# Windowed attention and a gated MLP on one core: casts of later pairs placed one slot sooner, and another order of the work at the head of two blocks

## The chip, the cores and the metric

The kernel runs on one core of a Trainium2 chip. A core has a matrix engine (PE, with its weight loads listed apart as PEld), three engines for elementwise work (DVE, ACT, POOL) and SP, which here only issues DMAs. Each engine works through its own queue in order, and the queues wait for each other by semaphores. The metric is the device time of one execution in microseconds (us); lower is better.

## The reference

Attention over 4 batches of 8 heads, 768 positions, head width 64, where a query sees the 128 latest positions and the first 4 ("sinks"); then, on the 512 columns that the heads make up together, a gated MLP whose gate mixes positions.

```python
scores = scale * np.matmul(q, k.transpose(0, 1, 3, 2))
keep = is_sink | in_window
scores = np.where(keep, scores, -1000000000.0)
a = np.exp(scores - max); a = a / (sum(a) + 1e-09)
x = heads_side_by_side(np.matmul(a, v))              # 4 x 768 x 512
h = gelu_tanh(x @ w_in)                              # 4 x 768 x 1024
u, v = h[..., :512], h[..., 512:]
v_n = (v - mean(v)) / np.sqrt(var(v) + 1e-06) * g_ln
v_s = np.einsum('ts,bsd->btd', w_sg, v_n) + b_sg[None, :, None]
out = x + (u * v_s) @ w_out
```

## The kernel before

The work is cut into 16 pairs of heads (numbered n; pair n belongs to batch n // 4) and 4 blocks of MLP, one for each batch b. In every batch there are six position tiles of 128.

For a pair, `load_all` brings k and q of pair n and v of pair n - 1 from memory through SP; `cast` (L101) turns them into bf16 on POOL; `columns` (L215) turns k and q so that the head width lies on partitions, with six PE transposes and a copy by ACT or DVE, while for the pairs from 12 on `columns_by_dma` (L228) has the DMA engines do it, issued by SP. `score` (L251) makes three groups of scores (g = 0, 1, 2), each one PSUM tile of two banks and one exponential on ACT. `keep_band` (L283) zeroes what lies outside the window: group 0 by a product with a mask on DVE, groups 1 and 2 by two selects each on POOL. `values` (L307) multiplies by v on PE, and DVE divides by the row sums into x. `turn_x` (L354) transposes x on PE and copies the result to xT by ACT or DVE; `turn_x_by_dma` does it by DMA. The scores and the products with v of a pair share two PSUM buffers (`ps_s`); all else that PE makes goes round four banks (`ps_m`).

For a block, `open_v` (L380) does three quarters of the product for one tile of the MLP's v half ahead of time, `hidden_v` (L390) the last quarter, the gelu on ACT and the batch statistics on DVE; `hidden_u` (L401) does the u half. Then DVE computes an inverse root in thirteen small steps and `normalise` (L436) writes vn. `hidden` (L594) runs six units of v and eight of u, with steps of other pairs placed after named units; unit numbers count from 0, so `LAST` is the last u unit. It leaves fourteen "fillers" behind: eight of `spatial` (L443; six products on PE, two DVE operations) and six of `project` (L475), one for each tile t. A projection's four products go to one bank, and the residual x is added either by DVE, or, for the tiles in `by_act`, by a fifth product with the identity on PE with a copy by ACT; SP sends the result out.

The order of everything is written by hand, as a string (`ORDER`, L723) and a table of steps placed inside the blocks (`INSIDE`, L718). The order in which steps stand there is the order of each engine's queue. The letters: `S n g..` scores, `m n g..` masks, `AV n` values, `KA`/`QA`/`QV n` columns of k or q with the copy on ACT or DVE, `TD n` columns by DMA, `XA`/`XV n` turn x with the copy on ACT or DVE, `XD n` by DMA, `ck`/`cq`/`cv n` casts on POOL, `L n` loads, `F c` the next c fillers, `O b j` open a tile of v of block b, `B b` the block's `hidden`. A "slot" below is the stretch from one pair's `S n 0 1` to the next pair's. k_bf, q_bf, kT and qT have two buffers each, the raw loads three of each kind, the exponentials three.

Of the kernel before, what the change touches and what calls it, by code (L numbers as in the profile page):

```python
# [18 lines left out]
def kernel(  # L19
# [14 lines left out]
    nc = tc.nc  # L34
    V, G, A = nc.vector, nc.gpsimd, nc.scalar

    B, H, S, Dh = q.shape
# [6 lines left out]
    HP = H // 2  # L44
# [103 lines left out]
    for i in range(WARM):  # L148
# [3 lines left out]
        out=halves[:, :, 0, :], in_=halves[:, :, 0, :], compare_op=ALU.is_ge, fill=DARK,  # L152
        base=0, pattern=[[0, 2], [1, 128]], channel_multiplier=-1)
    G.affine_select(
        out=halves[:, :, 1, :], in_=halves[:, :, 1, :], compare_op=ALU.is_ge, fill=DARK,
# [53 lines left out]
    def bank(shape, dtype, name):  # L209
        return ps_m.tile(shape, dtype, name=name, tag="m")  # L210

    kTs, qTs, exps, avs = {}, {}, {}, {}
    x_sb, xT = {}, {}
# [166 lines left out]
    def open_v(b, j, cs=range(KD - 1)):  # L380
        if j == 0 and 0 in cs:
            v_alls[b] = work.tile([128, NT, DF], F32, name="v_all", tag="v_all", bufs=1)
            mvs[b] = small.tile([128, NT, 2], F32, name="mv", bufs=2)
        if (b, j) not in hvs:
            hvs[b, j] = bank([128, 512], F32, "hv")
        for c in cs:
            nc.tensor.matmul(hvs[b, j], xT[b][:, c, 128 * j:128 * (j + 1)],  # L387
                             w_in_sb[:, c, DF:], start=(c == 0), stop=False)

    def hidden_v(b, j):  # L390
        if (b, j) not in hvs:
            open_v(b, j)
        h_ps, c = hvs.pop((b, j)), KD - 1
        nc.tensor.matmul(h_ps, xT[b][:, c, 128 * j:128 * (j + 1)],  # L394
                         w_in_sb[:, c, DF:], start=False, stop=True)
        A.activation(out=v_alls[b][:, j, :], in_=h_ps, func=AF.Gelu_apprx_tanh)  # L396
        st = small.tile([128, 6], F32, name="st")
        V.bn_stats(out=st, in_=v_alls[b][:, j, :])  # L398
        V.bn_aggr(out=mvs[b][:, j, :], in_=st)

    def hidden_u(b, f, n):  # L401
        if f == 0 and n == 0:
            uTs[b] = work.tile([128, KU, S], BF16, name="uT", bufs=1)
        h_ps = bank([128, 512], F32, "hu")
        for c in range(KD):
            nc.tensor.matmul(h_ps[:, 0:NH], w_in_sb[:, c, 128 * f:128 * (f + 1)],  # L406
                             xT[b][:, c, NH * n:NH * (n + 1)],
                             start=(c == 0), stop=(c == KD - 1))
        A.activation(out=uTs[b][:, f, NH * n:NH * (n + 1)],  # L409
                     in_=h_ps[:, 0:NH], func=AF.Gelu_apprx_tanh)  # L410
# [25 lines left out]
    def normalise(b, j):  # L436
        if j == 0:
            vns[b] = work.tile([128, NT, DF], BF16, name="vn", bufs=1)
        V.tensor_scalar(out=vns[b][:, j, :], in0=v_alls[b][:, j, :],  # L439
                        scalar1=mvs[b][:, j, 0:1], scalar2=rstds[b][:, j:j + 1],  # L440
                        op0=ALU.subtract, op1=ALU.mult)
# [30 lines left out]
                A.copy(o_sb, o_ps[:, 0:m])  # L472
            (nc.sync if eng is V else A).dma_start(out=out[b, rows, cols], in_=o_sb)

    def project(b, t, by_act):  # L475
        rows = slice(128 * t, 128 * (t + 1))
        o_ps = bank([128, 512], F32, "o_ps")
        o_sb = small.tile([128, DM], F32, name="o_sb", bufs=6)
        for c in range(KU):
            nc.tensor.matmul(o_ps, gTs[b][:, c, rows], w_out_sb[:, c, :],  # L480
                             start=(c == 0), stop=(c == KU - 1 and not by_act))
        if not by_act:
            V.tensor_add(o_sb.rearrange("p (h d) -> p h d", h=HP),
                         o_ps.rearrange("p (h d) -> p h d", h=HP), x_sb[b][:, :, t, :])
        else:
            nc.tensor.matmul(o_ps.rearrange("p (h d) -> p h d", h=HP), iden, x_sb[b][:, :, t, :],  # L486
                             start=False, stop=True)
        if by_act:
            A.copy(o_sb, o_ps)  # L489
        nc.sync.dma_start(out=out[b, rows, :], in_=o_sb)  # L490


    LEAST, MOST = 1e-20, 1e20
# [93 lines left out]
    fillers = []  # L587

    def fill(count=1):
        for _ in range(count):  # L590
            if fillers:
                fillers.pop(0)()

    def hidden(b, between):  # L594
        units = [lambda j=j: hidden_v(b, j) for j in range(NT)]
        units += [lambda f=f, n=n: hidden_u(b, f, n) for n in range(2) for f in range(KU)]
        after = {NT + 1: [lambda: inverse_root(b)]}
        for j in range(NT):
            after.setdefault(NT + 1 + j, []).append(lambda j=j: normalise(b, j))
        for i, unit in enumerate(units):  # L600
            unit()
            for step in after.get(i, []) + between.get(i, []):
                step()
        gate = [[lambda f=f, n=n: spatial(b, f, n) for f in range(KU)] for n in range(2)]
        if b < B - 1:
            fillers.extend(gate[0] + gate[1])
            by_act = (3, 5) if b == 0 else (5,) if b < B - 2 else (1, 3, 5)
            order = (0, 2, 4, 1, 3, 5) if b < B - 2 else (1, 0, 2, 3, 4, 5)
            fillers.extend(lambda t=t: project(b, t, t in by_act) for t in order)
            return  # L610

        rows = [lambda t=t: project(b, t, t != HT) for t in range(NT - 1)]
        fillers.extend(gate[0] + [gate[1][0], rows[0], gate[1][1], gate[1][2], rows[1],
                                  gate[1][3]] + rows[2:])
        fillers.append(lambda: project_last(b, NT - 1))
# [85 lines left out]
    for j in range(3):  # L701
# [12 lines left out]

    LAST = NT + 2 * KU - 1
    INSIDE = {  # L718
        1: {2: "AV 8", 5: "KA 9", 6: "L 12, L 13", 7: "QA 9", 9: "XD 8",
            LAST: "S 9 0 1, F 1, QV 10, F 1"},  # L720
        2: {2: "AV 12", 6: "L 15, L 16", 9: "XD 12", LAST: "S 13 0 1, F 2"},
    }
    ORDER = """  # L723
        S 4 0 1, W 3 4 5, m 4 0 1, F 1, KA 5, QV 5, F 1, S 4 2, m 4 2, ck 6, cq 6, cv 5, F 1,
# [2 lines left out]
        L 9, S 6 0 1, m 6 0 1, F 1, KA 7, AV 5, S 6 2, m 6 2, F 1, QA 7, ck 8, cq 8, cv 7, F 1,  # L727
        XV 5,
        L 10, S 7 0 1, m 7 0 1, F 1, KA 8, AV 6, QA 8, S 7 2, m 7 2, ck 9, cq 9, cv 8, F 1,
        L 11, S 8 0 1, m 8 0 1, XV 6, F 1, AV 7, S 8 2, m 8 2, ck 10, cq 10, cv 9,  # L730
        O 1 0, O 1 1, XV 7, O 1 2, B 1,
        m 9 0 1, F 1, KA 10, F 1, S 9 2, m 9 2, ck 11, cq 11, cv 10, F 1,
        S 10 0 1, m 10 0 1, F 1, AV 9, XD 9, S 10 2, m 10 2, ck 12, cq 12, KA 11, TD 12, L 14,
        F 1, QA 11, cv 11, F 1,
        S 11 0 1, m 11 0 1, F 1, AV 10, S 11 2, m 11 2, ck 13, cq 13, TD 13, F 1, cv 12, F 1,
        XV 10,
        S 12 0 1, m 12 0 1, F 1, AV 11, S 12 2, m 12 2, ck 14, cq 14, TD 14, F 1, cv 13, F 1,
        O 2 0, O 2 1, XV 11, O 2 2, B 2,
        ck 15, cq 15, m 13 0 1, F 2, S 13 2, m 13 2, TD 15, cv 14, F 1,
        S 14 0 1, m 14 0 1, F 1, AV 13, XD 13, S 14 2, m 14 2, F 1, cv 15, F 1,  # L740
        S 15 0 1, m 15 0 1, F 1, AV 14, S 15 2, m 15 2, F 1, G, F 1
    """

    def run(order):
        for step in order.split(","):
            op, *n = step.split()
            n = [int(i) for i in n]
            if op == "S":
                score(*n)
            elif op == "m":  # L750
                for g in n[1:]:
                    keep_band(n[0], g, V if g == 0 else G)
            elif op == "F":
                fill(n[0])
            elif op == "AV":
                values(n[0], 0, 1)
            elif op in ("ck", "cq", "cv"):
                cast(n[0], op[1], G)
            elif op in ("KA", "QA", "KV", "QV"):
                columns(n[0], op[0].lower(), A if op[1] == "A" else V)  # L760
            elif op == "TD":
                columns_by_dma(n[0])
            elif op == "XD":
                turn_x_by_dma(n[0])
            elif op in ("XV", "XA"):
                turn_x(n[0], A if op == "XA" else V)
            elif op == "L":
                load_all(n[0])
            elif op == "W":
                for si in n:  # L770
                    turn_weights(si, V)
            elif op == "O":
                open_v(*n)
            elif op == "G":
                draw_gelu()
            else:
                assert op == "B"
                hidden(n[0], {i: [lambda o=o: run(o)] for i, o in INSIDE[n[0]].items()})

    run(ORDER)  # L780
    values(NP - 1, 0)
    fill()
# [8 lines left out]
    hidden(B - 1, {2: [lambda: seen.update(c=count_good())],  # L791
                   LAST: [lambda: fill(3)]})
    seen["t"] = total(seen["c"])
# [41 lines left out]
```

## Time and profile before

| | us |
|---|---|
| median of 3 runs | 166.66 (166.65 to 174.25) |
| the profiled execution | 166.74 |
| its span, first to last instruction | 165.0 |
| DVE busy | 131.0 |
| ACT busy | 108.6 |
| POOL busy | 78.6 |

The mean granted PE clock was 0.997 of full speed. In a row of the timeline stand the start, the busy time, the engine, the line and operation, what it writes and reads, and how many instructions are merged in it; brackets give the engine's idle time before it and what ended that. A row of SP tells when SP issued a DMA and how long it was held there, not when the data landed. A row of the waits has the sum, the number and the longest of a group of waits. Busy times of PE overlap: a matmul's end is modelled, so the distance between starts tells the rate. Some matmul records are missing.

### The profile page before, as it was taken

Reading aid. Unit: us, or ns where it says so; the run is one execution under the profiler, and the core shown is the slowest. Engines: PE = TensorE matmul, PEld = TensorE weight load, DVE = VectorE, ACT = ScalarE, POOL = GpSimd, SP = SyncE. Lnnn points to the kernel's source line nnn. Section 1 sums busy time; section 2 is a strip of 40 time slices with the busy share of each in tenths; the row PEclk is TensorE's granted clock in tenths of the full one; section 3 lists DMA queues with packets and bytes.
Section 4 is the critical chain, followed back from the end, with each engine's and each line's share of the span. In section 5 each row is a group of like instructions: output and inputs, shape, how many; then the busy total and the mean of one; then the engine's idle time right before and its main releaser. Section 6 shows DMA issues by size and latency. Waiting matters only on the chain.

```text
span 165.0 us, 4407 instructions
## 1 busy us (share of the span) xinstructions
PE 152.3 (92%) x1734; PEld 90.7 (55%) x1752; DVE 131.0 (79%) x302; ACT 108.6 (66%) x147; POOL 78.6 (48%) x113
## 2 busy tenths in 40 slices
PE   3899999999999999999999899999999999999950
PEld 3555574666576655565566456553565645555430
DVE  6787975996899978799778965989999859997520
ACT  3189888889968796698878285679548457511220
POOL 6568771206899979500299997023775000000000
PEclk9999999999999999999999999999999999999998
DMA  4999979999999999999602699999626310050352
GB/s 136 333 346 248 203 107 274 212 316 310 294 232 309 306 315 360 267 214 216 132 30 52 131 237 107 343 225 217 179 48 52 127 68 0 0 190 6 126 183 89
DMA packets 60195, 31.11 MB, mean 189 GB/s; under 512 B 48356, under 2 KB 57080, under 8 KB 60168
## 3 DMA queue, kind: packets, MB, share of 16 engines
q1 hardware_dynamic: 56800, 27.47, 70.1%
q0 software_dynamic: 2944, 2.77, 10.3%
q10 hardware_dynamic: 424, 0.53, 0.9%
q8 instruction: 15, 0.25, 0.6%
q14 instruction: 12, 0.10, 0.2%
HBM read 24.81 MB, written 6.29 MB: 188 GB/s over the span
## 4 chain that ended last, share of the span: by engine, by line
PE 68%; DVE 15%; POOL 5%; ACT 4%; issue 3%; DMA 2%; ACTq 0%; POOLq 0%
PE vs L449 16%; PE hu L406 10%; PE o_ps L480 8%; PE hv L387 7%; PE sc L267 6%; PE av L331 5%; ACT ex L281 3%; PE hv L394 3%; PE kps L219 2%; DVE st L398 2%; PE xps L358 2%; PE qps L219 2%; DVE vn L439 2%; DVE x L343 2%; DVE vsink L160 2%
## 5 line engine op out<-in xcount | busy, mean ns | idle before, releaser
L281 ACT ACTIVATE ex<-sc 128x1024 bf16<-128x1024 f32 x48 | 47.6, 1024 | 17.4 <-PE sc L277 7.4
L449 PE MATMUL vs<-wsgT,vn 128*128 128x384 bf16 x192 | 36.1, 327 | 0.4
L298 POOL TENSOR_SCALAR_AFFINE_SELECT ex<-ex 128x512 bf16<-128x512 bf16 x24 | 16.1, 670 | 21.1 <-ACT ex L281 19.3
L449 PEld LDWEIGHTS <-vn 128*128 128x128 bf16 x192 | 17.2, 98 | 13.2 <-DVE vn L439 1.5
L480 PE MATMUL o_ps<-w_out_sb,gT 128*128 128x512 bf16 x83 | 22.5, 380 | 0.5
L107 POOL CAST k_bf<-k_sb 128x768 bf16<-128x768 f32 x15 | 12.9, 861 | 20.4 <-DMA k_sb<-in_k_dram 15.5
L452 DVE SCALAR_TENSOR_TENSOR gv<-vs,g_sb,b_bc 128x384 bf16<-128x384 f32 x32 | 19.6, 611 | 3.4 <-PE vs L449 2.7
L406 PE MATMUL hu<-xT,w_in_sb 128*128 128x384 bf16 x128 | 22.1, 326 | 0.0
L396 ACT ACTIVATE v_all<-hv 128x512 f32<-128x512 f32 x24 | 13.2, 599 | 9.1 <-PE hv L394 9.0
L398 DVE BATCH_NORM_STATS2 st<-v_all 128x6 f32<-128x512 f32 x24 | 16.1, 669 | 3.5 <-ACT v_all L396 3.5
L387 PE MATMUL hv<-w_in_sb,xT 128*128 128x512 bf16 x67 | 18.2, 379 | 0.3 <-issue 0.2
L409 ACT ACTIVATE uT<-hu 128x384 bf16<-128x384 f32 x32 | 15.7, 492 | 4.1 <-PE hu L406 3.7
L267 PE MATMUL sc<-qT,kT 64*128 64x256 bf16 (+2 forms) x384 | 16.1, 256 | 1.9 <-DMA qT<-q_bf 0.8
L290 DVE TENSOR_TENSOR ex<-ex,mask 128x1024 bf16<-128x1024 bf16 x15 | 14.3, 955 | 4.2 <-ACT ex L281 4.1
L107 POOL CAST q_bf<-q_sb 128x768 bf16<-128x768 f32 x15 | 14.9, 996 | 3.7 <-DMA q_sb<-in_q_dram 3.4
L104 POOL CAST v_sb<-v_sb 128x768 bf16<-128x768 f32 x16 | 15.2, 951 | 3.0 <-DMA v_sb<-in_v_dram 2.9
L406 PEld LDWEIGHTS <-w_in_sb 128*128 128x128 bf16 x128 | 12.3, 98 | 8.0
L331 PEld LDWEIGHTS <-ex 128*128 128x128 bf16 x352 | 12.5, 98 | 3.7 <-ACT ex L281 1.8
L455 DVE TENSOR_TENSOR gT<-gv,uT 128x384 bf16<-128x384 bf16 x32 | 12.9, 404 | 1.9
L331 PE MATMUL av<-v_sb,ex 128*128 128x65 bf16 x352 | 14.2, 194 | 0.1
L489 ACT COPY o_sb<-o_ps 128x512 f32<-128x512 f32 x10 | 5.8, 588 | 12.8 <-PE o_ps L486 11.3
L300 POOL TENSOR_SCALAR_AFFINE_SELECT ex<-ex 128x512 bf16<-128x512 bf16 (+1 forms) x24 | 13.7, 569 | 0.0
(92 smaller groups left out, 221.1 us busy)
## 6 DMA issues: line engine op xcount, KB each, us to landing
k_sb<-in_k_dram SPq DMA_DIRECT2D x16, 384.0 KB, 6.9
v_sb<-in_v_dram SPq DMA_DIRECT2D x16, 384.0 KB, 6.0
out_dram<-o_sb SPq DMA_DIRECT2D x23, 256.0 KB, 2.7
q_sb<-in_q_dram SPq DMA_DIRECT2D x15, 384.0 KB, 5.3
wsg_sb<-in_moe_w_sg_dram POOLq DMA_DIRECT2D x2, 576.0 KB, 11.3
w_in_sb<-in_moe_w_in_dram POOLq DMA_DIRECT2D x2, 256.0 KB, 5.3
w_in_sb<-in_moe_w_in_dram POOLq DMA_DIRECT2D x1, 512.0 KB, 5.4
w_out_sb<-in_moe_w_out_dram POOLq DMA_DIRECT2D x1, 512.0 KB, 9.3
```

What stands on the lines that cost most here:

```text
L107: eng.tensor_copy(dst.rearrange("p t (h d) -> p h t d", h=2), src)
L267: nc.tensor.matmul(sc[part, 512 * l + w:512 * l + w + n_q], kT[rows, 128 * j + wide * a:128 * j + wide * (a + 1)], qT[rows, 128 * j:128 * ...
L281: A.activation(out=exps[n][:, g, :], in_=sc, func=AF.Exp, scale=scale)
L298: eng.affine_select(out=diag, in_=diag, compare_op=ALU.is_ge, fill=0.0, base=0, pattern=[[0, 2], [0, 2], [1, 128]], channel_multiplier=-1)
L331: nc.tensor.matmul(av[:, m, l, :], probs(j, l, half), v_sb[:, l, j, :], start=first, stop=False)
L387: nc.tensor.matmul(hvs[b, j], xT[b][:, c, 128 * j:128 * (j + 1)], w_in_sb[:, c, DF:], start=(c == 0), stop=False)
L398: V.bn_stats(out=st, in_=v_alls[b][:, j, :])
L406: nc.tensor.matmul(h_ps[:, 0:NH], w_in_sb[:, c, 128 * f:128 * (f + 1)], xT[b][:, c, NH * n:NH * (n + 1)], start=(c == 0), stop=(c == KD - 1))
L409: A.activation(out=uTs[b][:, f, NH * n:NH * (n + 1)], in_=h_ps[:, 0:NH], func=AF.Gelu_apprx_tanh)
L449: nc.tensor.matmul(vs[:, 0:NH], vns[b][:, si, 128 * f:128 * (f + 1)], wsgT[:, si, cols], start=(si == 0), stop=(si == NT - 1))
L452: V.scalar_tensor_tensor(out=gv, in0=vs[:, 0:NH], scalar=g_sb[:, f:f + 1], in1=b_bc[:, cols], op0=ALU.mult, op1=ALU.add)
L480: nc.tensor.matmul(o_ps, gTs[b][:, c, rows], w_out_sb[:, c, :], start=(c == 0), stop=(c == KU - 1 and not by_act))
```

## The change

- In `project`, the end (residual and output DMA) becomes an inner function that can be kept for later: step `D` runs the next filler's products and keeps its end, step `E` runs that end.
- At the head of block 1 (pairs 6, 7, 8): x of pair 6 is turned with the copy on ACT (`XA 6` for `XV 6`), the residual of the projection beside it comes after `AV 7`, and the mask of group 0 of pair 8 after the turn of x of pair 7. At the head of block 2 the mask of group 0 of pair 12 likewise comes after the turn of x of pair 11.
- `AV 8` and `AV 12` come one unit later in their blocks.
- The casts of k and q of pairs 11 to 14 and of v 10 stand about one slot sooner: pair 11 and v 10 inside block 1 at `LAST`, pair 12 in the slot of pair 9, pair 13 in that of pair 10, pair 14 in that of pair 11. The casts of v 11, 12 and 13 keep their places. k of pair 15 stays, q of pair 15 comes after the masks of groups 0 and 1 of pair 13.
- In block 1 the residual of tile 3 goes from DVE to PE and ACT, as it is in block 0.

```diff
-    def project(b, t, by_act):
+    def project(b, t, by_act, ends=None):
...
-        if not by_act:
-            V.tensor_add(o_sb.rearrange("p (h d) -> p h d", h=HP),
-                         o_ps.rearrange("p (h d) -> p h d", h=HP), x_sb[b][:, :, t, :])
-        else:
+        if by_act:
             nc.tensor.matmul(o_ps.rearrange("p (h d) -> p h d", h=HP), iden, x_sb[b][:, :, t, :],
                              start=False, stop=True)
-        if by_act:
-            A.copy(o_sb, o_ps)
-        nc.sync.dma_start(out=out[b, rows, :], in_=o_sb)
+        def end():
+            if by_act:
+                A.copy(o_sb, o_ps)
+            else:
+                V.tensor_add(o_sb.rearrange("p (h d) -> p h d", h=HP),
+                             o_ps.rearrange("p (h d) -> p h d", h=HP), x_sb[b][:, :, t, :])
+            nc.sync.dma_start(out=out[b, rows, :], in_=o_sb)
+        if ends is None:
+            end()
+        else:
+            ends.append(end)
...
-            by_act = (3, 5) if b == 0 else (5,) if b < B - 2 else (1, 3, 5)
+            by_act = (3, 5) if b < B - 2 else (1, 3, 5)
...
-        1: {2: "AV 8", 5: "KA 9", 6: "L 12, L 13", 7: "QA 9", 9: "XD 8",
-            LAST: "S 9 0 1, F 1, QV 10, F 1"},
-        2: {2: "AV 12", 6: "L 15, L 16", 9: "XD 12", LAST: "S 13 0 1, F 2"},
+        1: {3: "AV 8", 5: "KA 9", 6: "L 12, L 13", 7: "QA 9", 9: "XD 8",
+            LAST: "ck 11, cq 11, cv 10, S 9 0 1, F 1, QV 10, F 1"},
+        2: {3: "AV 12", 6: "L 15, L 16", 9: "XD 12", LAST: "S 13 0 1, F 2"},
...
-        L 11, S 8 0 1, m 8 0 1, XV 6, F 1, AV 7, S 8 2, m 8 2, ck 10, cq 10, cv 9,
-        O 1 0, O 1 1, XV 7, O 1 2, B 1,
-        m 9 0 1, F 1, KA 10, F 1, S 9 2, m 9 2, ck 11, cq 11, cv 10, F 1,
-        S 10 0 1, m 10 0 1, F 1, AV 9, XD 9, S 10 2, m 10 2, ck 12, cq 12, KA 11, TD 12, L 14,
-        F 1, QA 11, cv 11, F 1,
-        S 11 0 1, m 11 0 1, F 1, AV 10, S 11 2, m 11 2, ck 13, cq 13, TD 13, F 1, cv 12, F 1,
+        L 11, S 8 0 1, m 8 1, XA 6, D, AV 7, E, S 8 2, m 8 2, ck 10, cq 10, cv 9,
+        O 1 0, O 1 1, XV 7, m 8 0, O 1 2, B 1,
+        m 9 0 1, F 1, KA 10, F 1, S 9 2, m 9 2, ck 12, cq 12, F 1,
+        S 10 0 1, m 10 0 1, F 1, AV 9, XD 9, S 10 2, m 10 2, KA 11, TD 12, L 14,
+        F 1, QA 11, cv 11, ck 13, cq 13, F 1,
+        S 11 0 1, m 11 0 1, F 1, AV 10, S 11 2, m 11 2, TD 13, F 1, cv 12, ck 14, cq 14, F 1,
         XV 10,
-        S 12 0 1, m 12 0 1, F 1, AV 11, S 12 2, m 12 2, ck 14, cq 14, TD 14, F 1, cv 13, F 1,
-        O 2 0, O 2 1, XV 11, O 2 2, B 2,
-        ck 15, cq 15, m 13 0 1, F 2, S 13 2, m 13 2, TD 15, cv 14, F 1,
+        S 12 0 1, m 12 1, F 1, AV 11, S 12 2, m 12 2, TD 14, F 1, cv 13, F 1,
+        O 2 0, O 2 1, XV 11, m 12 0, O 2 2, B 2,
+        ck 15, m 13 0 1, cq 15, F 2, S 13 2, m 13 2, TD 15, cv 14, F 1,
...
+            elif op == "D":
+                fillers.pop(0)(ends)
+            elif op == "E":
+                ends.pop()()
```

More of the change, by code (lines that the diff above doesn't have):

```diff
@@ L606, in hidden @@
             fillers.extend(gate[0] + gate[1])
-            by_act = (3, 5) if b == 0 else (5,) if b < B - 2 else (1, 3, 5)
+            by_act = (3, 5) if b < B - 2 else (1, 3, 5)
             order = (0, 2, 4, 1, 3, 5) if b < B - 2 else (1, 0, 2, 3, 4, 5)
-            fillers.extend(lambda t=t: project(b, t, t in by_act) for t in order)
+            fillers.extend(lambda ends=None, t=t: project(b, t, t in by_act, ends) for t in order)
             return
@@ L742 @@
     """
+    ends = []
     def run(order):
```

## The prediction

> **What bounds the kernel now.** First the page's busy times, then the waits sorted by waiter with PE's own.
>
> ```profile
> PE 152.3 (92%) x1734; PEld 90.7 (55%) x1752; DVE 131.0 (79%) x302; ACT 108.6 (66%) x147; POOL 78.6 (48%) x113
> ...
> PE sc L267 <- DMA qT<-q_bf: 0.8, 1, 0.8
> ...
> PE xps L358 <- DVE x L343: 0.3, 1, 0.3
> ...
> PEld L449 <- DVE vn L439: 1.5, 5, 0.4
> ```
>
> PE is busy 152.3 of 165.0 us, so only a gap in its stream is worth time, and an edit elsewhere pays only by closing one. Three of PE's gaps lie where the change works: before the turn of x of pair 7 (head of block 1), before the scores of pair 12 (a DMA transpose of q), and in the first spatial products after block 2 (vn). The timeline shows each. Its busy times overrun the true step, so I take steps from start to start.
>
> Head of block 1, PE, then DVE, then ACT:
>
> ```profile
> 62.31 0.40 PE L338 MATMUL av<-vsink,ex 128*128 128x65 bf16 x4
> ...
> 63.21 1.24 PE L387 MATMUL hv<-w_in_sb,xT 128*128 128x512 bf16 x5 [0.16 <-issue]
> 64.70 0.51 PE L358 MATMUL xps<-iden,x 128*128 128x128 bf16 x6 [0.25 <-DVE x L343]
> 65.05 0.81 PE L387 MATMUL hv<-w_in_sb,xT 128*128 128x512 bf16 x3
> ...
> 61.40 1.06 DVE L290 TENSOR_TENSOR ex<-ex,mask 128x1024 bf16<-128x1024 bf16 x1 [1.09 <-ACT ex L281]
> 62.38 0.54 DVE L367 COPY xT<-xps 128x768 bf16<-128x768 bf16 x1
> 62.84 0.67 DVE L483 TENSOR_TENSOR o_sb<-o_ps,x 128x512 f32<-128x512 f32 x1
> 63.44 0.21 DVE L342 RECIPROCAL rcps<-av 128x12 f32<-128x12 f32 x1
> 63.69 0.96 DVE L343 TENSOR_TENSOR x<-av,rcps 128x768 bf16<-128x768 f32 x1
> ...
> 66.75 0.69 DVE L398 BATCH_NORM_STATS2 st<-v_all 128x6 f32<-128x512 f32 x1 [0.87 <-ACT v_all L396]
> ...
> 60.34 1.94 ACT L281 ACTIVATE ex<-sc 128x1024 bf16<-128x1024 f32 x2 [0.29 <-issue]
> 63.15 1.02 ACT L281 ACTIVATE ex<-sc 128x1024 bf16<-128x1024 f32 x1 [0.87 <-PE sc L277]
> ...
> 129.77 0.80 ACT L365 COPY xT<-xps 128x768 bf16<-128x768 bf16 x1 [0.67 <-PE xps L358]
> ```
>
> The hv steps are (1.24 - 0.38)/4 = 0.215 us apart, so after five PE is free at 63.21 + 5 x 0.215 = 64.29; the sixth of the two opened banks has no record and fits before 63.21. PE waits until 64.70: **0.41 us**, for x of pair 7. That x is late because DVE does mask (61.40), turned x (62.38) and residual (62.84) first, although AV 7 ends at 62.31 + 0.40 = 62.71.
>
> Between blocks 1 and 2, POOL, SP, the chain of waits, and PE:
>
> ```profile
> 79.72 0.64 POOL L298 TENSOR_SCALAR_AFFINE_SELECT ex<-ex 128x512 bf16<-128x512 bf16 x1 [11.34 <-ACT ex L281]
> ...
> 84.03 0.82 POOL L107 CAST k_bf<-k_sb 128x768 bf16<-128x768 f32 x1
> ...
> 89.23 0.98 POOL L107 CAST k_bf<-k_sb 128x768 bf16<-128x768 f32 x1
> 90.16 1.29 POOL L107 CAST q_bf<-q_sb 128x768 bf16<-128x768 f32 x1
> ...
> 87.48 1.22 SPq L371 DMA_TRANSPOSE xT<-x  x1
> 90.23 1.21 SPq L233 DMA_TRANSPOSE kT<-k_bf  x1
> 91.54 1.25 SPq L233 DMA_TRANSPOSE qT<-q_bf  x1
> ...
> 93.47 0.65 SPq L95 DMA_DIRECT2D q_sb<-in_q_dram  x1
> ...
> 91.54 2.77 DMA qT<-q_bf
> ...
> 93.19 0.50 PE L358 MATMUL xps<-iden,x 128*128 128x128 bf16 x6
> 94.44 0.61 PE L267 MATMUL sc<-qT,kT 64*128 64x256 bf16 x8 [0.75 <-DMA qT<-q_bf]
> ```
>
> POOL casts k of pair 12 at 89.23 and q at 90.16; SP, which was free from 87.48 + 1.22, sends the transposes only then, and q lands at 91.54 + 2.77 = 94.31. Six transposes take 65.05 - 64.70 = 0.35 of PE, so PE was free at 93.54 and waited to 94.44: **0.90 us**. Before 79.72 POOL had idled 11.34 us.
>
> Block 2 (and vn and the first products of block 1 for comparison), DVE, POOL, PE, ACT:
>
> ```profile
> 75.22 2.83 DVE L439 TENSOR_SCALAR vn<-v_all,mv,y 128x512 bf16<-128x512 f32 x6
> 110.38 0.73 DVE L431 TENSOR_TENSOR s<-y 128x6 f32<-128x6 f32 x1
> 111.55 3.46 DVE L439 TENSOR_SCALAR vn<-v_all,mv,y 128x512 bf16<-128x512 f32 x6
> ...
> 110.27 0.83 POOL L107 CAST k_bf<-k_sb 128x768 bf16<-128x768 f32 x1 [7.71 <-DMA k_sb<-in_k_dram]
> 112.08 0.83 POOL L107 CAST q_bf<-q_sb 128x768 bf16<-128x768 f32 x1 [0.98 <-DMA q_sb<-in_q_dram]
> ...
> 78.86 1.14 PE L449 MATMUL vs<-wsgT,vn 128*128 128x384 bf16 x6
> 102.11 0.83 PE L331 MATMUL av<-v_sb,ex 128*128 128x65 bf16 x22
> 113.18 0.38 PE L486 MATMUL o_ps<-x,iden 128*128 128x512 bf16 x1
> 113.40 2.98 PE L449 MATMUL vs<-wsgT,vn 128*128 128x384 bf16 x12
> 120.76 2.12 PE L449 MATMUL vs<-wsgT,vn 128*128 128x384 bf16 x12
> ...
> 116.81 1.02 ACT L281 ACTIVATE ex<-sc 128x1024 bf16<-128x1024 f32 x1 [1.59 <-PE sc L277]
> ```
>
> Twelve spatial products take 2.12 us undisturbed and 2.98 here: **0.86 us** of waiting for vn. And vn took 3.46 against 2.83 in block 1, with the cast of q 15 (112.08 to 112.91) in the midst of it.
>
> **Block 1's head, part by part.** XA 6: the copy goes to ACT at 0.80 (row 129.77) and stands behind two exponentials that end at 60.34 + 1.94 = 62.28, so it ends at 63.08. Queued behind it is the exponential of S 8 2, which started at 63.15 anyway. PE needs this copy for the third hv step, near 63.42, 0.3 later: cost nothing; without that cover at most the 0.80. D and E: PE's four products stay, the residual moves behind x. DVE is then free when AV 7 ends: reciprocal near 62.75, and with its row's step of 0.25 x runs 63.00 to 63.96. PE turns pair 7 at 64.29 without waiting: the whole 0.41 goes. The residual then runs 63.96 to 64.63, and its bank is the one that O 1 2 takes at 64.29 + 0.35 = 64.64; next late is that, by 0.0 to 0.1. Its output DMA is issued about 1.1 later, and behind it on SP the loads of pairs 12 and 13; the first of them is cast at 84.03 today, which covers it. The copies of x of pair 7 started 0.55 after its transposes (64.70, and hv follows at 65.05), the mask of 8 0 now follows them: 64.84 + 0.62 for two halves + 1.06 = 66.5. Who waits for the mask: AV 8, which follows hv blocks 0 to 2 and is now one block later: 65.05 + 6 x 0.215 - 0.41 + 4 x 0.215 = 66.8, and the first batch statistics, which ran at 66.75 and could start 0.41 sooner, so DVE's chain to vn gains 0.25, not 0.41. The x of AV 8 and its turn by DMA move with it; they are wanted only in block 2. PE reads vn from 78.86, after DVE's end at 75.22 + 2.83 = 78.05. Gain 0.41, bounds 0 (a bank or the ACT copy is late) and 0.41.
>
> **Casts one slot sooner.** Pair 11 and v 10 are cast in the end of block 1, in POOL's idle 11.34 us. Pair 12 then stands where pair 11 stood, at 84.03, done 0.98 + 1.29 later at 86.3. SP sends x of pair 9 at 87.48 - 0.41 = 87.07 and then, at its step of 1.3 (90.23 to 91.54), k of 12 at 88.4 and q at 89.7, which lands 2.77 later at 92.5. PE comes there at 93.54 - 0.41 = 93.13, so the 0.90 goes with 0.6 to spare; next late is nothing within 0.6. The loads of pair 14 and v 13, the next on SP, move up by 1.9 too. Bounds 0 (the transposes land no sooner) and 0.90; I take 0.90, since SP was seen waiting for a cast alone.
>
> The added wait: the casts of pair 14 now stand ahead of masks 12 1 and 12 2 on POOL and wait for loads that were issued shortly before. Behind them are these masks and the cast of v 13, and AV 12 waits for the masks. Weighed as a rival below.
>
> **Block 2's head.** The mask of 12 0 falls in the gap ahead of the first statistics, of which block 1 shows 0.87; at 0.69 to 1.06 it costs the chain 0 to 0.19. Residual t = 3 of block 1 leaves DVE (-0.67, after vn, so no one on the chain waits for it) and becomes one more matmul on PE, 113.40 - 113.18 = **+0.22 us**, and one more ACT copy. That copy costs nothing: bounded by the 0.80 of the copy above, it fits the 1.59 that ACT idles before 116.81; without this cover, the exponential of S 13 2 would be up to 0.80 later. Cast q 15 goes behind mask 13 1 and out of vn's way. With the 1.31 gained so far vn starts at 111.55 - 1.31 + 0.19 = 110.43 and ends 2.83 later at 113.26; PE starts at 113.40 - 1.31 + 0.22 = 112.31 and reads the last of six 5 x 0.163 later at 113.12 (0.163 is (2.12 - 0.33)/11). So 0.14 of waiting stays of 0.86: gain 0.86 - 0.14 - 0.22 = 0.50. Bounds: 0.64 with no wait left, -0.13 if vn still takes 3.46 (113.89, waiting 0.77).
>
> A rule speaks against moving casts beside DVE's chain. Row 110.38 first: a 128x6 product took 0.73 until 111.11, where the cast begun at 110.27 ended (111.10), and vn stretched beside a cast. The Trainium skill, page SBUF — State Buffer, section SBUF: two separate sides, says that DVE's two-port modes and GpSimd share a port pair as an exclusive lock, the loser blocking for the whole instruction. By that rule each moved cast could hold block 1's chain for its full length; the trace agrees in block 2, by 3.46 - 2.83 = 0.63 for one cast.
>
> **Sum.** 0.41 + 0.90 + 0.50 = 1.81, bounds -0.13 and 1.95. After block 2 PE's stream has no edit but order, so the gain goes through to the end. The profiled execution took 166.74 (span 165.0): 164.93. It stands 0.08 above the median of 166.66, so **164.9 us**.
>
> **Rivals.**
> 1. The transposes of pair 12 land no sooner, because the DMA rings and not SP hold them. For it: one landing of 2.77 is all that is seen, behind one other transpose; in the new order there are two. Against: SP's rows show it idle until the cast. 164.9 + 0.9 = 165.8.
> 2. The moved casts lock out block 1's chain. Three at up to 0.98 are 2.9; the slack is PE's sixth read at 78.86 - 0.41 + 5 x 0.163 = 79.27 less vn's end at 78.05 - 0.25 = 77.80, so 1.5. At worst 1.4 late: 166.3; with two casts, 2.0 - 1.5 = 0.5: 165.4. Against: batch statistics take most of that time, and the cast at 110.27 cost less than the 0.73 of the row that it held.
> 3. Slower: q of pair 14 holds POOL. After it lands come a cast of up to 1.29 and four mask pieces of up to 0.64, 3.85 together; AV 12 comes at 102.11 + 0.86 - 1.31 = 101.66. So it decides from a landing at 97.8. Its issue at 93.47 - 1.86 = 91.6 and the median landing,
> ```profile
> q_sb<-in_q_dram SPq DMA_DIRECT2D x15, 384.0 KB, 5.3
> ```
> give 96.9, 0.9 inside. Landing at 100.1, 8.5 after issue, would cost 2.3: 167.2.
> 4. It doesn't do what it says: the gaps close and open again a step later, at the exponentials. 166.7.
> 5. More: with DVE and POOL ahead, smaller waits after pair 12 go as well: 164.2.
>
> **Chances.** Forecast 0.62 (own range 164.5 to 165.3), rivals 0.12, 0.10, 0.06, 0.04, 0.06. The range 164.2 to 166.3 leaves out the slower one, no gain and half of the fifth. Within 2%, about what a measurement of this kernel can tell from no change, means 163.3 to 170.0: faster beyond it needs 1.6 more than the sum, nearly twice, 0.04; slower needs pair 14 five us late, 0.03; within 0.93.
>
> **What would show it.** In the changed profile: PE's wait of xps on x gone in block 1 and DVE's order AV 7's x, residual, copies, mask; three casts on POOL between 68 and 79; SP sending pair 12 right behind x of 9, and no PE wait for qT; vn of block 2 near 2.83 and its twelve products near 2.3. Wrong would be: POOL idle before a cast of pair 14 with AV 12 late; vn of block 1 ending after 79; a new PE gap at O 1 2.

## The result and the profile after

The changed kernel takes 165.28 us (median; 164.95 to 165.75 in the eight executions that the ratio uses) where the kernel before takes 166.65 in the same session. The ratio is 0.992, with a 95% interval of 0.9894 to 0.9947: a gain of 1.4 us where 1.8 had been forecast, and by the 2% mark no change. Some executions here run about 2% or more long, nearly all of them at a lower granted clock; the ratios leave these out, and of the three profiles that fell on one (block 1 alone, the first deferral, the changed kernel a third time) only the order of events is used.

The profiled execution of the changed kernel took 165.75 us (span 164.0), the longest of those eight. From its waits (waiter, line, what it waited for, sum, number, longest):

```profile
PEld L449 <- DVE vn L439: 0.6, 2, 0.4
PE xps L358 <- DVE x L343: 0.5, 1, 0.5
...
PE sc L267 <- DVE x L343: 0.3, 1, 0.3
```

Of the three waits that the change was about, the one for q of pair 12 is gone from the list and the one for vn fell from 1.5 to 0.6. But a wait of the x turn for DVE's x is still there, 0.5 where it was 0.3. It is another one: not in block 1, but thirty microseconds later.

**Head of block 1.** The timeline of the changed kernel, PE, DVE, and then POOL, DVE and PE at the block's end:

```profile
63.08 1.47 PE L387 MATMUL hv<-w_in_sb,xT 128*128 128x512 bf16 x6
64.39 0.50 PE L358 MATMUL xps<-iden,x 128*128 128x128 bf16 x6
...
62.84 0.23 DVE L342 RECIPROCAL rcps<-av 128x12 f32<-128x12 f32 x1 [2.44 <-PE av L338]
63.11 0.96 DVE L343 TENSOR_TENSOR x<-av,rcps 128x768 bf16<-128x768 f32 x1
63.98 0.68 DVE L491 TENSOR_TENSOR o_sb<-o_ps,x 128x512 f32<-128x512 f32 x1
...
72.56 0.83 POOL L104 CAST v_sb<-v_sb 128x768 bf16<-128x768 f32 x1
...
72.69 0.72 DVE L425 TENSOR_SCALAR si<-w 128x6 int32<-128x6 int32 x1
...
75.45 2.83 DVE L439 TENSOR_SCALAR vn<-v_all,mv,y 128x512 bf16<-128x512 f32 x6
...
78.54 1.14 PE L449 MATMUL vs<-wsgT,vn 128*128 128x384 bf16 x6
```

DVE has nothing ahead of x of pair 7, which runs from 63.11. The six hv steps begin at 63.08 and end at 63.08 + 6 x 0.215 = 64.37, and the transposes follow at 64.39: the 0.41 us are gone. One of the three casts that came into this block, v 10 at 72.56, does hold a step of DVE's chain (0.72 where its neighbours take 0.17). vn still ends at 78.28, and PE reads the last of its six tiles at 78.54 + 5 x 0.163 = 79.36, so 1.1 us were left to spare.

**The slots of pairs 10 and 11.** PE, DVE, POOL and SP:

```profile
91.99 1.03 PE L481 MATMUL o_ps<-w_out_sb,gT 128*128 128x512 bf16 x4
93.53 0.51 PE L358 MATMUL xps<-iden,x 128*128 128x128 bf16 x6 [0.51 <-DVE x L343]
93.97 0.61 PE L267 MATMUL sc<-qT,kT 64*128 64x256 bf16 x8
...
88.85 0.96 DVE L455 TENSOR_TENSOR gT<-gv,uT 128x384 bf16<-128x384 bf16 x1
89.74 1.30 DVE L290 TENSOR_TENSOR ex<-ex,mask 128x1024 bf16<-128x1024 bf16 x1
...
91.61 0.73 DVE L455 TENSOR_TENSOR gT<-gv,uT 128x384 bf16<-128x384 bf16 x1
...
92.52 0.96 DVE L343 TENSOR_TENSOR x<-av,rcps 128x768 bf16<-128x768 f32 x1
...
88.78 0.82 POOL L107 CAST k_bf<-k_sb 128x768 bf16<-128x768 f32 x1
89.55 0.95 POOL L107 CAST q_bf<-q_sb 128x768 bf16<-128x768 f32 x1
...
88.44 1.21 SPq L233 DMA_TRANSPOSE kT<-k_bf  x1
89.75 2.22 SPq L233 DMA_TRANSPOSE qT<-q_bf  x1
```

SP sends k and q of pair 12 at 88.44 and 89.75 (88.4 and 89.7 were forecast), and the scores of pair 12 at 93.97 wait for nothing. But one step ahead of them PE was free at 91.99 + 4 x 0.215 = 92.85 and began the transposes of pair 10 at 93.53: **0.68 us**, for x of pair 10. Three of DVE's operations before that x are long: a product of 0.96 and a mask of 1.30 while POOL casts k and q of pair 13, and a product of 0.73 beside a mask piece on POOL (91.50, 0.63). The first two end behind POOL's cast by their own undisturbed length (0.36 and 0.69 in the profile with pair 13's casts put back, below) less 0.15: the cast of k ends at 88.78 + 0.82 = 89.60 and the product at 89.81, 0.21 later; the cast of q at 90.50 and the mask at 91.04, 0.54 later. The Trainium skill, page SBUF — State Buffer, section SBUF: two separate sides, says that a DVE operation with two SBUF inputs and a GpSimd operation (POOL here) that reads SBUF share a port pair as an exclusive lock, which whichever starts first holds for its whole instruction. Product and mask have two SBUF inputs each; the trace agrees but for those 0.15 us, and the runs below show the other outcome too.

**Block 2.** DVE, POOL and PE:

```profile
101.09 1.23 DVE L290 TENSOR_TENSOR ex<-ex,mask 128x1024 bf16<-128x1024 bf16 x1
...
111.23 2.83 DVE L439 TENSOR_SCALAR vn<-v_all,mv,y 128x512 bf16<-128x512 f32 x6
...
98.03 0.83 POOL L107 CAST q_bf<-q_sb 128x768 bf16<-128x768 f32 x1 [0.94 <-DMA q_sb<-in_q_dram]
...
102.51 0.84 PE L331 MATMUL av<-v_sb,ex 128*128 128x65 bf16 x22
...
113.15 2.28 PE L449 MATMUL vs<-wsgT,vn 128*128 128x384 bf16 x12
```

vn is back at 2.83, and twelve spatial products take 2.28 where 2.12 is undisturbed: 0.16 of waiting is left, 0.14 had been forecast. From the first scores of pair 12 to the third group of pair 13's the lead over the kernel before grows from 0.47 us (94.44 to 93.97) to 0.95 (116.31 to 115.36).

The books: 0.41 + 0.90 - 0.68 + 0.48 = 1.11 us. The profiled executions differ by 166.74 - 165.75 = 0.99. That is 0.82 short of the forecast of 1.81, and 0.68 of it is this wait.

### The profile page after: what moved, and what is told of

It reads as the page before. It is cut to its first block, busy times and chain, and to the rows that moved or that the text cites. A ratio compares the mean times of both kernels' runs of the same rounds, so it can differ in the third digit from the quotient of the medians.

```text
span 164.0 us, 4426 instructions
## 1 busy us (share of the span) xinstructions
PE 153.6 (94%) x1753; PEld 90.8 (55%) x1753; DVE 132.6 (81%) x300; ACT 109.6 (67%) x149; POOL 77.2 (47%) x113
## 4 chain that ended last, share of the span: by engine, by line
PE 83%; DVE 9%; ACT 3%; issue 1%; ACTq 0%
PE vs L449 18%; PE hu L406 13%; PE o_ps L481 10%; PE hv L387 10%; PE sc L267 7%; PE av L331 6%; PE hv L394 3%; PE xps L358 3%; PE kps L219 3%; ACT ex L281 3%; PE qps L219 2%; PE av L338 2%; PE sc L247 2%; DVE vsink L160 2%; DVE ex L290 2%; PE o_ps L484 1%
## 5 line engine op out<-in xcount | busy, mean ns | idle before, releaser
L298 POOL TENSOR_SCALAR_AFFINE_SELECT ex<-ex 128x512 bf16<-128x512 bf16 x24 | 16.6, 690 | 17.2 <-ACT ex L281 14.6
L481 PE MATMUL o_ps<-w_out_sb,gT 128*128 128x512 bf16 x92 | 23.2, 380 | 0.0
L387 PE MATMUL hv<-w_in_sb,xT 128*128 128x512 bf16 x72 | 18.8, 379 | 0.0
L455 DVE TENSOR_TENSOR gT<-gv,uT 128x384 bf16<-128x384 bf16 x32 | 15.0, 469 | 1.9
L107 POOL CAST q_bf<-q_sb 128x768 bf16<-128x768 f32 x15 | 14.2, 945 | 4.6 <-DMA q_sb<-in_q_dram 2.3
L290 DVE TENSOR_TENSOR ex<-ex,mask 128x1024 bf16<-128x1024 bf16 x15 | 15.1, 1004 | 1.2 <-ACT ex L281 1.0
L104 POOL CAST v_sb<-v_sb 128x768 bf16<-128x768 f32 x16 | 14.5, 905 | 2.6 <-DMA v_sb<-in_v_dram 2.5
L481 PEld LDWEIGHTS <-gT 128*128 128x128 bf16 x92 | 8.3, 98 | 8.8 <-issue 0.8
```

Source lines behind the costliest of these rows:

```text
L107: eng.tensor_copy(dst.rearrange("p t (h d) -> p h t d", h=2), src)
L290: V.tensor_mul(ex[:, :, 0:w], ex[:, :, 0:w], m[:, 0:w].unsqueeze(1).to_broadcast([128, 2, w]))
L298: eng.affine_select(out=diag, in_=diag, compare_op=ALU.is_ge, fill=0.0, base=0, pattern=[[0, 2], [0, 2], [1, 128]], channel_multiplier=-1)
```

## The experiments

Theory A is that the new wait comes from the casts of pair 13, which now stand beside the DVE work that leads to x of pair 10. Its rivals B and C stand in the first expectation.

**One part at a time.** Pair 13's casts go back to where they were, and all else stays changed:

```diff
-        F 1, QA 11, cv 11, ck 13, cq 13, F 1,
+        F 1, QA 11, cv 11, F 1,
-        S 11 2, m 11 2, TD 13,
+        S 11 2, m 11 2, ck 13, cq 13, TD 13,
```

> The changed kernel with one part undone: k and q of pair 13 are cast where they were before, after the masks of pair 11, all else as changed. In the changed kernel PE waited 0.68 us for x of pair 10, and DVE's steps ahead of that x were long (1.30 for the mask of pair 11, 0.96 and 0.73 for two products that take 0.36 elsewhere) while POOL cast pair 13. Theory A (the cast and DVE hold each other up): mask near 0.7 to 0.8, both products near 0.36, x of pair 10 about 1 us sooner, PE's wait on it under 0.1, and the scores of pair 12 follow at once: 0.6 to 0.7 us faster than the changed kernel, span near 163.3. Theory B (x is no longer late, but q of pair 12 still lands near 93.5): the wait moves to the scores of pair 12, 0.3 to 0.5 us long; 0.2 to 0.4 faster than the changed kernel. Theory C (x is late by the order of DVE's queue, not by POOL): the mask and products stay long and the wait of 0.68 stays; no difference.

Ratio 0.9911 (0.9877 to 0.9945). Its timeline, DVE, POOL, PE:

```profile
88.81 0.36 DVE L455 TENSOR_TENSOR gT<-gv,uT 128x384 bf16<-128x384 bf16 x1
89.60 0.69 DVE L290 TENSOR_TENSOR ex<-ex,mask 128x1024 bf16<-128x1024 bf16 x1 [0.43 <-ACT ex L281]
...
93.17 0.95 POOL L107 CAST k_bf<-k_sb 128x768 bf16<-128x768 f32 x1
...
92.81 0.50 PE L358 MATMUL xps<-iden,x 128*128 128x128 bf16 x6
93.24 0.61 PE L267 MATMUL sc<-qT,kT 64*128 64x256 bf16 x8
```

Product and mask are short, and neither the transposes nor the scores of pair 12 wait. The casts now begin at 93.17, when x is done. That is what theory A expected, and B and C lose by it; nothing else became late in the wait's place. One profile without the wait is no proof by itself, as the second one of the changed kernel below shows, but here pair 13 is not cast beside that DVE work at all. The time that was expected is seen in the profile only: the profiled execution, 165.11, is 0.64 us shorter than the changed kernel's, but by the ratios (0.9911 and 0.992) the two kernels are some 0.15 us apart and not 0.6.

The next three make one part of the change each, on the kernel before.

The head of block 1 alone (all casts and block 2 as before):

```diff
-        1: {2: "AV 8",
+        1: {3: "AV 8",
...
-        L 11, S 8 0 1, m 8 0 1, XV 6, F 1, AV 7, S 8 2, m 8 2, ck 10, cq 10, cv 9,
-        O 1 0, O 1 1, XV 7, O 1 2, B 1,
+        L 11, S 8 0 1, m 8 1, XA 6, D, AV 7, E, S 8 2, m 8 2, ck 10, cq 10, cv 9,
+        O 1 0, O 1 1, XV 7, m 8 0, O 1 2, B 1,
```

> The kernel before with only the new order at the head of block 1 (x of pair 6 copied by ACT, deferred residual, mask of pair 8 behind the turn of x, AV 8 one unit later). If the parts add up: PE's wait of 0.41 for x of pair 7 goes, nothing takes it back, 0.4 us faster than before (166.25). Rival: the gain is absorbed by the next wait, the DMA transpose of q of pair 12, which grows from 0.90 to 1.3; time as before.

Ratio 0.9964 (0.9947 to 0.9981), 0.6 us. In the profile the wait for x of pair 7 is gone, and the one for q of pair 12 stays. What is gained in block 1 is kept; the forecast of 0.4 lies inside the interval (0.3 to 0.9).

The casts alone:

```diff
-            LAST: "S 9 0 1, F 1, QV 10, F 1"},
+            LAST: "ck 11, cq 11, cv 10, S 9 0 1, F 1, QV 10, F 1"},
...
-        S 9 2, m 9 2, ck 11, cq 11, cv 10, F 1,
+        S 9 2, m 9 2, ck 12, cq 12, F 1,
...
-        S 10 2, m 10 2, ck 12, cq 12, KA 11, TD 12, L 14,
-        F 1, QA 11, cv 11, F 1,
+        S 10 2, m 10 2, KA 11, TD 12, L 14,
+        F 1, QA 11, cv 11, ck 13, cq 13, F 1,
...
```

> The kernel before with only the casts of pairs 11 to 14 and of v 10 moved. If the casts that now run beside DVE give back what the earlier transposes win: the wait for q of pair 12 (0.90) goes and a wait of 0.5 to 0.8 for x of pair 10 comes, 0.1 to 0.4 us faster than before. As predicted on record for this part: 0.90 faster. Rival, the casts in block 1 hold up its DVE chain so that PE waits for vn: as before or slower.

Ratio 0.995 (0.9927 to 0.9972), 0.8 us. In the profiled execution the wait for q of pair 12 is gone, and the transposes of pair 10 begin 0.69 late (PE was free at 92.58 + 4 x 0.215 = 93.44), after a product of 0.97 and a mask of 1.30. PE:

```profile
94.13 0.51 PE L358 MATMUL xps<-iden,x 128*128 128x128 bf16 x6 [0.51 <-DVE x L343]
```

PE's last matmul starts 0.02 sooner than in the kernel before, or 0.28 when the 0.26 by which this execution was already late at the scores of pair 8 is taken off. The forecast of 0.90 less 0.68 is 0.22. The timed executions gained more than that, and more than the 0.1 to 0.4 expected.

The edits of block 2 alone:

```diff
-            by_act = (3, 5) if b == 0 else (5,) if b < B - 2 else (1, 3, 5)
+            by_act = (3, 5) if b < B - 2 else (1, 3, 5)
...
-        2: {2: "AV 12",
+        2: {3: "AV 12",
...
-        S 12 0 1, m 12 0 1, F 1, AV 11,
+        S 12 0 1, m 12 1, F 1, AV 11,
...
-        O 2 0, O 2 1, XV 11, O 2 2, B 2,
+        O 2 0, O 2 1, XV 11, m 12 0, O 2 2, B 2,
-        ck 15, cq 15, m 13 0 1, F 2,
+        ck 15, m 13 0 1, cq 15, F 2,
...
```

> The kernel before with only the edits around block 2 (residual of tile 3 by PE and ACT, mask of pair 12 behind the turn of x of pair 11, AV 12 one unit later, q of pair 15 cast after the first masks of pair 13). On record for this part: vn back from 3.46 to 2.83, PE's waits for vn from 0.86 to about 0.14, one more matmul of 0.22: 0.50 us faster than before. Rival: vn stays long for another reason than the cast of q 15: 0.2 slower than before.

Ratio 0.9983 (0.9961 to 1.0004), which by itself shows no gain. The trace does: its twelve products take 2.11 us, with no wait, and PE's last matmul starts at 158.25 where it started at 158.76, 0.51 sooner (0.48 without the 0.03 by which it was ahead at the scores of pair 8). And the trace shows one thing more. The casts of this kernel stand as in the kernel before, with pair 12 where the changed kernel has pair 13. POOL, DVE, PE:

```profile
89.09 0.82 POOL L107 CAST k_bf<-k_sb 128x768 bf16<-128x768 f32 x1
...
89.14 0.98 DVE L455 TENSOR_TENSOR gT<-gv,uT 128x384 bf16<-128x384 bf16 x1
90.05 1.30 DVE L290 TENSOR_TENSOR ex<-ex,mask 128x1024 bf16<-128x1024 bf16 x1
...
93.47 0.51 PE L358 MATMUL xps<-iden,x 128*128 128x128 bf16 x6
94.52 0.61 PE L267 MATMUL sc<-qT,kT 64*128 64x256 bf16 x8 [0.55 <-DMA qT<-q_bf]
```

The same long product and long mask, and x of pair 10 late by 0.3 (PE was free at 92.30 + 4 x 0.215 = 93.16); the next product, which took 0.73 in the changed kernel, takes 0.36 here, and POOL's next cast is the long one (1.28). The 0.3 cost nothing, because the scores right behind wait for q of pair 12 anyway. In the profile of the kernel before, DVE was ahead at the same place (DVE; POOL's casts followed at 89.23 and 90.16):

```profile
89.17 0.36 DVE L455 TENSOR_TENSOR gT<-gv,uT 128x384 bf16<-128x384 bf16 x1
89.96 0.79 DVE L290 TENSOR_TENSOR ex<-ex,mask 128x1024 bf16<-128x1024 bf16 x1 [0.43 <-ACT ex L281]
```

So the meeting of casts and DVE is older than the change, and the wait that the change removed had covered it.

**The changed kernel once more**, with no edit:

> The changed kernel itself, beside the others on one chip. Its profile tells whether PE's wait for x of pair 10 (0.68 in the first profile) is there each time. If it is the fixed meeting of casts and DVE steps: 0.6 to 0.7 again, and this kernel is 0.6 us slower than the one with the casts of pair 13 back. If the meeting is a matter of chance from run to run: between 0 and 0.7, and the two kernels' times overlap.

Median 165.07, ratio 0.9917 (0.9883 to 0.9951). The profiled execution took 164.71 us, 2.03 less than that of the kernel before, and has no wait of the transposes. DVE, POOL, PE:

```profile
89.01 0.36 DVE L455 TENSOR_TENSOR gT<-gv,uT 128x384 bf16<-128x384 bf16 x1
89.81 0.79 DVE L290 TENSOR_TENSOR ex<-ex,mask 128x1024 bf16<-128x1024 bf16 x1 [0.44 <-ACT ex L281]
...
89.05 1.01 POOL L107 CAST k_bf<-k_sb 128x768 bf16<-128x768 f32 x1
90.00 1.28 POOL L107 CAST q_bf<-q_sb 128x768 bf16<-128x768 f32 x1
...
92.16 1.03 PE L481 MATMUL o_ps<-w_out_sb,gT 128*128 128x512 bf16 x4
93.02 0.50 PE L358 MATMUL xps<-iden,x 128*128 128x128 bf16 x6
```

Here the product started at 89.01, 0.04 us before the cast at 89.05; in the first profile the cast (88.78) was 0.07 ahead of the product (88.85). The one that comes second pays: POOL with 1.01 and 1.28, which nobody waits for, or DVE with 0.96, 1.30 and 0.73, for which PE waits 0.68. PE's last matmul starts 1.58 us sooner than in the kernel before, 1.82 when the 0.24 by which it was late at the scores of pair 8 is taken off, beside the 1.81 of the forecast. That the two agree to 0.01 is partly chance, since the parts miss in both directions: the lead is 0.99 + 0.24 = 1.23 at the scores of pair 12, where 1.31 was forecast, and block 2 adds 0.65, where 0.50 was.

**POOL taken out, and more of POOL.** In the first of these runs ACT casts k and q of pair 13, behind the exponential of `S 11 2`:

```diff
-        eng.tensor_copy(...)
+        (eng.copy if eng is A else eng.tensor_copy)(...)
...
-        F 1, QA 11, cv 11, ck 13, cq 13, F 1,
+        F 1, QA 11, cv 11, F 1,
-        S 11 2, m 11 2, TD 13,
+        S 11 2, m 11 2, cK 13, cQ 13, TD 13,
...
+            elif op in ("cK", "cQ"):
+                cast(n[0], op[1].lower(), A)
```

> The changed kernel with k and q of pair 13 cast by ACT, behind the exponential of pair 11's last group, in the 2.35 us that ACT idles there; POOL does not cast them at all. If it is POOL's casts that hold up DVE: mask and products short as with the casts back on POOL in their old place, no wait for x of pair 10, 0.6 to 0.7 us faster than the changed kernel. If the reading of the raw loads by any engine holds it up, or ACT's extra 1.6 to 2 us push the exponentials of pair 12 out: a new wait of PE for ACT of 0.2 to 0.8 and no gain.

Ratio 0.989 (0.9853 to 0.9927). DVE:

```profile
88.75 0.36 DVE L455 TENSOR_TENSOR gT<-gv,uT 128x384 bf16<-128x384 bf16 x1
89.54 0.69 DVE L290 TENSOR_TENSOR ex<-ex,mask 128x1024 bf16<-128x1024 bf16 x1 [0.43 <-ACT ex L281]
```

Product and mask are short, and neither the transposes nor the scores of pair 12 wait. ACT casts later than POOL did, from 91.99 to 93.54, so this run takes POOL out but does not test ACT's reading beside these two operations. By the ratios it is not 0.6 to 0.7 us faster than the changed kernel (0.989 and 0.9917, 0.4 us apart and inside each other's intervals). The second is the kernel with pair 13's casts put back, once more, beside the changed one in the same session:

> The changed kernel with the casts of pair 13 back, again, for a comparison on the same chip as the changed kernel: 0.6 to 0.7 us faster than it if the wait for x of pair 10 is a fixed one.

Median 164.92, ratio 0.9906 (0.9871 to 0.9941), its trace as at first. It and the changed kernel (165.07) are 0.15 apart, inside their intervals, and not the 0.6 to 0.7 of a wait that is there each time.

Then each cast of pair 13 was done twice, in the changed kernel, to the same result:

```diff
-        eng.tensor_copy(...)
+        for _ in range(2 if n == 13 else 1):
+            eng.tensor_copy(...)
```

> The changed kernel with each of the two casts of pair 13 done twice in its place, to the same tile with the same values: the suspected cost doubled, 1.7 us more on POOL between two masks. If POOL's casts hold up DVE's steps ahead of x of pair 10: the wait of PE for that x is there in the profile, 0.6 or more whichever side starts first, and the scores of pair 12 follow it at once. If x of pair 10 is late for another reason: no more wait than in the changed kernel's other profiles (0 or 0.68); what is lost then is lost where PE waits for the masks of pair 11, at the product with v of pair 11.

There are too few executions for a ratio; the profiled one took 164.84. Its timeline (one added line moves the line numbers by one), DVE and POOL:

```profile
88.73 0.36 DVE L456 TENSOR_TENSOR gT<-gv,uT 128x384 bf16<-128x384 bf16 x1
89.53 0.79 DVE L291 TENSOR_TENSOR ex<-ex,mask 128x1024 bf16<-128x1024 bf16 x1 [0.44 <-ACT ex L282]
...
88.78 2.23 POOL L108 CAST k_bf<-k_sb 128x768 bf16<-128x768 f32 x2
90.96 1.87 POOL L108 CAST q_bf<-q_sb 128x768 bf16<-128x768 f32 x2
```

The expectation failed: twice the casts, and PE does not wait for x of pair 10. The product was 0.05 ahead, and DVE stayed ahead. With DVE ahead, then, even doubled casts cost PE nothing; what they cost with POOL ahead, this run does not show.

**The changed kernel a third time**, and **the casts without pair 13** on the kernel before (pairs 11, 12, 14 and v 10 moved, pair 13 left). The edit of the second, against the casts alone:

```diff
-        F 1, QA 11, cv 11, ck 13, cq 13, F 1,
+        F 1, QA 11, cv 11, F 1,
-        S 11 2, m 11 2, TD 13,
+        S 11 2, m 11 2, ck 13, cq 13, TD 13,
```

> The changed kernel a third time. Two profiles of it differ by 1.04 us, 0.68 of it in PE's wait for x of pair 10, which hangs on whether POOL's cast of k 13 or DVE's product beside it starts first (0.07 and 0.04 us apart). If that is so: this profile shows either the wait with the cast first or no wait with the product first, and nothing between.

> The kernel before with the casts of pairs 11, 12, 14 and of v 10 moved as in the change, and pair 13 left where it was. If the term of the prediction for the casts was right but for the meeting of pair 13 with DVE: no wait for q of pair 12 and none for x of pair 10, PE 0.90 us ahead at the scores of pair 12, 0.8 to 0.9 us faster than before in each profile. If the transposes of pair 12 hold PE in any case: a wait of 0.3 or more stays there, 0.5 faster or less.

The first: ratio 0.9939 (0.9909 to 0.9969). In its profile the product started at 96.05, the cast at 96.08, and nothing waited for x: again the first to start goes undelayed. The second: ratio 0.9953 (0.9934 to 0.9972), 0.8 us. Its PE, and in the last row the last matmul of the kernel before:

```profile
93.24 0.50 PE L358 MATMUL xps<-iden,x 128*128 128x128 bf16 x6
93.67 0.61 PE L267 MATMUL sc<-qT,kT 64*128 64x256 bf16 x8
...
157.85 0.27 PE L471 MATMUL o_ps<-x,iden 128*128 128x256 bf16 x1
...
158.76 0.27 PE L471 MATMUL o_ps<-x,iden 128*128 128x256 bf16 x1
```

Neither transposes nor scores wait, and the last matmul starts at 157.85 where it started at 158.76: 0.91 us (0.96 with the 0.05 by which it was later at the scores of pair 8). This is the term of 0.90, alone and undiminished. The ratio, though, is that of the casts with pair 13 (0.995), so the timed executions do not show the loss of 0.68 that the profile of those had.

**An attempt at more.** Before the scores of pair 8 PE waits for x of pair 6, in both kernels: in the changed one four products begin at 58.61 and are through at 58.61 + 4 x 0.215 = 59.47, and the scores start at 59.95, 0.48 later. On top of the kernel with pair 13's casts put back, the residual of a projection that DVE does ahead of that x was put off, in two runs of one kernel:

```diff
-        S 7 0 1, m 7 0 1, F 1, KA 8, AV 6, QA 8,
+        S 7 0 1, m 7 0 1, D, KA 8, AV 6, E, QA 8,
```

> The changed kernel with the casts of pair 13 back, and besides the residual of the projection in pair 7's slot deferred behind x of pair 6, as the change does it one slot later. PE waits 0.46 to 0.48 for x of pair 6 before the scores of pair 8 in every profile so far; one residual of 0.68 stands ahead of that x. If the same remedy works: that wait goes, 0.45 us faster than the kernel with the casts back. Rival: the scores of pair 8 then wait for the exponential of pair 7's last group, or the bank kept longer stops PE: under 0.2.

> Casts of pair 13 back and the residual in pair 7's slot deferred behind x of pair 6, again. In its first profile the wait for x of pair 6 was gone but the second half of the scores of pair 8 waited 0.39 for the exponential of pair 7's last group. If that holds: a wait of about 0.4 there, and 0.0 to 0.1 us gained on the kernel with the casts back. If that first profile misled: no wait there, 0.45 gained.

Ratios 0.9897 (0.9855 to 0.9938) and 0.9931 (0.9899 to 0.9963), so no faster than without it. The second profile, PE:

```profile
59.64 0.38 PE L481 MATMUL o_ps<-w_out_sb,gT 128*128 128x512 bf16 x1
59.95 0.39 PE L267 MATMUL sc<-qT,kT 64*128 64x256 bf16 x4
60.57 0.40 PE L267 MATMUL sc<-qT,kT 64*128 64x256 bf16 x4 [0.23 <-ACT ex L281]
```

The scores start without waiting for x, and their second half then waits for an exponential. Eight such scores take 0.54 up to the next operation (93.67 to 94.21 with the casts but pair 13), so four take 0.27, and the second half is 60.57 - 59.95 - 0.27 = 0.35 late; with the 59.95 - 59.64 - 0.215 = 0.10 ahead of the first it is 0.45 where it was 0.48. The stall only moved. With the casts done twice the same two waits are seen without the deferral, in another split (0.16 and 0.31), so that it was the deferral that moved it is not shown.

## Why the prediction held, and where it fell short

- **PE sets the time, and only its gaps are worth anything.** Right: the lead that each part gains at its gap is still there at PE's last matmul (0.96 with the casts but pair 13, 0.48 with block 2, both against the scores of pair 8).
- **Block 1, 0.41.** Right, and DVE's order is the one forecast. The rival that moved casts lock out the chain to vn came true for one step of 0.55 (0.72 for 0.17), where 2.9 had been its bound. It went into the slack, of which 1.1 was left.
- **Casts, 0.90.** Right in mechanism and in size where pair 13 stays out. SP sent pair 12 within 0.1 us of the times forecast, and with pair 13's casts put back the scores of pair 12 start at 93.24 without waiting, so the rival that the DMA rings hold it falls.
- **The step that failed: "next late is nothing within 0.6".** The 0.6 was q's lead alone. Next late was x of pair 10, and only where POOL's cast starts just ahead of DVE's product: then 0.68 is lost (0.3 in the profile of block 2 alone, with pair 12's casts at that place). The forecast had the sign in hand: in the rows of the kernel before, the casts of pair 12 at that place take 0.98 and 1.29, where a cast alone takes 0.82. They were read as the price of a cast; beside DVE's rows (89.17 and 89.96) they show POOL coming second to DVE. Had POOL come first, DVE would have paid, and the 0.90 us of waiting for q that the change takes away would no longer have covered it. The exclusive lock was weighed for block 1, where casts were new, and not here, where one pair's casts took the place of another's.
- **Block 2, 0.50.** Right in mechanism. From the first scores of pair 12 to the third group of pair 13's it gained 0.48 in the changed kernel's first profile, and 0.65, at the upper bound of 0.64, in its second and with block 2 alone, where PE does not wait for vn in these twelve products. The mask before the first statistics took 1.23 beside a cast, above its bound of 1.06; vn started at 111.23, 0.12 behind the 110.43 + 0.68 that the forecast and the new wait make.
- **The slower rival, q of pair 14 holding POOL.** The load was late by its own reckoning: SP issued it at 92.64 where 91.6 had been forecast, after holding the transpose of q of pair 12 for 2.22 us, and POOL's cast got it at 98.03, beyond the 97.8 from which it was to cost. But cast and masks behind it took 2.96 us, up to 100.99, and not the 3.85 of the upper rows, and AV 12 came at 102.51, 1.5 us later.

What stays open is how often each order comes up in the timed executions, of which no trace exists. In the eight profiles with casts at that place, of this kernel, its parts, and the kernel before, POOL was ahead three times, by 0.05 to 0.07 us, and DVE five times, by 0.03 to 0.06; product and mask were long in those three and short in those five. No edit here sets the order on purpose, so that it decides rests on these profiles. Times of the changed kernel and of the one with pair 13's casts put back overlap, so that the second is faster is not shown, nor that the meeting is what the timed executions of the changed kernel lost; the second is free of the meeting. The second too gained only 1.5 to 1.6 us by its ratios, with 1.8 inside the interval, so up to 0.3 us of the forecast has no cause shown here.

## What to carry to other kernels

When a stall goes, ask not only which input of the same step is next, but which steps just before it were late and hidden by it. A row that is longer than its fellows (here a cast of 0.98 or 1.29 instead of 0.82) can mark two engines that meet: price the meeting with the other engine losing, before taking away the wait that covers it. And where two orders are some tens of nanoseconds apart, look at more than one profile before explaining a difference.

## What the runs showed of the hardware

- In eight profiles the operation that started first, by 0.03 to 0.07 us, went undelayed (the product with 0.36, the cast with 0.82), and the other engine was held at more than one operation. DVE, when second, was held at three of its next four operations in two profiles (0.96, 1.30 and 0.73, where it takes 0.36, 0.79 and 0.36 when first) and at two in the third; the operation not held, which makes gv and reads one input from PSUM, takes 0.60 in either order. POOL, when second, was held at both casts (1.01 and 1.28).
- One kernel, at mean granted clocks of 0.990 and 0.991 in two profiles, took 165.75 and 164.71 us; 0.68 us of the difference is that one meeting.
- SP was held at the transpose of q of pair 12 for 1.25 us in the kernel before and for 2.22 and 1.71 in two profiles of the changed one; why is not known. PE did not wait for it, but the loads behind it on SP went out later than forecast.
